# Second-half x operands in four long units, their rests between the halves, scales' one-column matmuls elsewhere, two buffers for down weights

## The chip, the cores and the metric

The kernel runs on one core of a Trainium2 chip. The core has five engines that run side by side and are ordered only by semaphores: TensorE (PE in the profile; its weight loads are PEld), VectorE (DVE), ScalarE (ACT), GpSimd (POOL) and SyncE (SP), which in this kernel issues every DMA. Each engine takes its own instructions in the order in which the program issued them. Matmuls write to eight PSUM banks, and VectorE or ScalarE must read a bank before it can be written anew. The metric is the time of one execution in microseconds, lower is better.

## The reference

Two branches read the same x (2048 rows, 576 columns) and are mixed by a gate:

```python
x = A_x
g = _sigmoid((x * gate_w).sum(-1, keepdims=True))
a = _A_ref(x, A_wq, A_wk, A_wv, A_wo, A_beta)
b = _B_ref(x, B_w_gate, B_w_up, B_w_down)
return g * a + (1 - g) * b
```

Branch A is an attention of 32 heads of size 18 over four segments of 512 rows, with a softmax inside each segment and a running memory matrix from one segment to the next. Branch B is `(silu(x @ w_gate) * (x @ w_up)) @ w_down`, with 4608 inner columns. Everything is in float32, so the kernel splits operands into a high part (the value rounded to a narrower type) and a low part (what the rounding left), and multiplies high with high, high with low and low with high.

## The kernel before, in words

**Projections (0 to about 240 us).** For each of the four segments `s` the kernel makes nine q and k chains (`qk`, chain number `n` from 0 to 8), then eight value groups (`v_step`, group number `n` from 0 to 7) with the memory's matmuls (`mem_step`). `mid` is a list of small work that `qk` issues behind a chain's matmuls. Beside this the kernel measures how large x and the first weights are: squares and peaks are summed up in columns of the tile `sc`; `total` adds such columns, `power` sums over the partitions with a one-column matmul (line 139) into bank 7 and turns the result into a power of two by four small VectorE instructions, and `back` makes the inverse. `sx` is the scale of x; `sw[0]`, `sw[1]` ... are those of groups of four weight tiles. The transposes of the memory update (line 454) and every third value group use bank 7 too.

**Feed-forward (from about 240 us).** The inner columns are cut into 36 tiles, `f` = 0 to 35, and the rows into two halves of 1024. All 36 tiles are worked through for the first half, then for the second: 72 units in a list `seq`, numbered by `pos`. A unit forms gate and up products by Strassen's scheme: seven products (`seven`, `j` = 0 to 6; lines 1188 and 1191) of seven combinations of the weights with seven combinations of x, so 49 matmuls. The last 64 of the 576 columns are handled as a rest, by line 1191. After every third unit the down products of three tiles are due, 16 groups of nine matmuls (line 993, evicted into the sum `ya` by VectorE in line 1002), and they are issued in the following unit, the one with `f % 3 == 0`. That unit is therefore long (about 36 us in the first half), the two behind it are short (about 11). The attention of branch A (`att_gen`: scores in lines 823 and 870, exponentials on ScalarE in line 874, a second part on POOL in line 962) is issued in the long units only while the first half lasts.

**Order of the work.** It is written out by hand. A unit has eight beats (`tick`). `defer(k, fn)` hangs work on the k-th beat from now, so a plan `(o, fn)` in a unit runs at the end of beat `o` (counted from 0; 8 and more lie in the next units). At a beat, what is due goes to its engine's queue in the order in which it was hung there. Between the halves stand ten more beats (`BREAK`), in which nothing but the last 16 down groups is issued.

**What the change touches.** The second half needs its own x operands: for each of seven combinations and two row blocks `z` of the contraction a high part (ScalarE, float16) and a low part (VectorE, line 127), from loaded x tiles that POOL's subtractions (line 1136) combine in place. `x_second` (from `pos` 27) loads four tiles for `z` = 0 and then four for `z` = 1, and spreads the steps over 18 beats each, so over a long unit and the two short ones after it; `parts` issues high and low part in the same beat. `rest_second` (from `pos` 24) does the same for the rests (lines 195 and 196, POOL in line 1159). The raw tiles lie in free places of the x operands' tiles; one of `z` = 1 takes one of the four buffers of `raw_tile`, through which the weights are loaded (`w_load`, line 254). The down weights are loaded by `d_load` (line 259) into the tile `draw`, split by ScalarE and VectorE (`d_split`, lines 974 and 975) and stored.

## Time and profile before

| | |
|---|---|
| median of 3 runs | 1795.76 us (1792.91 to 1799.9) |
| the profiled execution's own time | 1797.75 us |
| its span, first to last instruction | 1795.8 us |
| mean granted TensorE clock | 0.992 |
| PE busy / PEld busy | 1745.5 us (97%) / 1233.4 us (69%) |
| DVE busy / ACT busy / POOL busy | 1347.3 us (75%) / 1005.4 us (56%) / 850.8 us (47%) |
| chain that ended last | PE 78%, DVE 7%, ACT 5% |
| second half's x operands made | in units 24 to 32, 682 to 887 us |

Names in the rows are those of the program: `xo` and `xr` are x tiles (whole ones and rests), `ya` the sum of the down products, `hh` and `hl` the high and low part of a unit's result, `wo__` numbers the weight parts, `kst` and `qst` the attention's keys and queries. A row `A <- B` in the waits says how long engine A stood idle until B's instruction had ended. In a row by stretch, busy time and instruction count stand for each engine, and the clock is the share of full speed that TensorE was granted. A group by line shows busy time and mean nanoseconds of one instruction, and behind the second bar the idle time just before such instructions.

### The profile page before, as it was taken

The numbers are of one execution on the slowest core, as the hardware profiler recorded it, in microseconds if no ns is written. First come the engines' busy times: TensorE is split into PE (matmuls) and PEld (weight loads), VectorE is DVE, ScalarE is ACT, GpSimd is POOL, SyncE is SP. The second block draws the span as 40 slices with busy tenths as digits, with TensorE's granted clock in tenths as the row PEclk, the third lists the DMA queues.
The fourth block names the chain that finished last, engine by engine and source line by source line (L and its number), as shares of the span: only waits on it lengthen the run. The fifth ranks groups of instructions, "written<-read, shape, count | busy, mean of one in ns | idle before, by whom it ended". The sixth has DMA issues, their size and how long they took to land.

```text
span 1795.8 us, 35846 instructions
## 1 busy us (share of the span) xinstructions
PE 1745.5 (97%) x12401; PEld 1233.4 (69%) x12401; DVE 1347.3 (75%) x3339; ACT 1005.4 (56%) x1740; POOL 850.8 (47%) x1065
## 2 busy tenths in 40 slices
PE   9999999999999999988999999999999999999999
PEld 7888856656766676555566757766766766766699
DVE  6768776778878877886775887787877778775455
ACT  7756575767676765664653554455455455455411
POOL 3325551335544554564442555555556555555121
PEclk9999999999999999999999999999999999999999
DMA  8654475776677655544535343354344344333544
GB/s 286 217 189 160 148 250 188 224 224 198 172 239 230 214 174 173 189 134 121 177 115 175 109 147 112 93 156 123 89 134 144 93 120 146 101 103 121 166 143 139
DMA packets 228100, 288.82 MB, mean 161 GB/s; under 512 B 87952, under 2 KB 145168, under 8 KB 227920
## 3 DMA queue, kind: packets, MB, share of 16 engines
q1 hardware_dynamic: 227920, 286.54, 50.3%
q8 instruction: 98, 1.61, 0.4%
q14 instruction: 82, 0.67, 0.1%
HBM read 188.63 MB, written 97.81 MB: 160 GB/s over the span
## 4 chain that ended last, share of the span: by engine, by line
PE 78%; DVE 7%; ACT 5%; issue 3%; DMA 3%; POOL 2%; SPq 1%; DVEq 0%; ACTq 0%; POOLq 0%
PE bank L1188 32%; PE bank L993 23%; PE bank L170 7%; PE bank L1191 5%; PE bank L823 4%; PE bank L870 4%; PE bank L899 2%; PE bank L901 1%; POOL q L399 1%; SPq L936 1%; DMA kst<-stk 1%; DMA rc<-rt 1%; ACT L1181 0%; DMA draw<-in_wd_dram 0%; DVE xo L127 0%
## 5 line engine op out<-in xcount | busy, mean ns | idle before, releaser
L993 PE MATMUL bank<-dw,hh 128*128 128x320 f32 (+1 forms) x2304 | 509.2, 313 | 10.1 <-DVE ya L1002 9.1
L962 POOL TENSOR_TENSOR p<-pe,p 128x512 f16<-128x512 f32 x320 | 386.0, 1206 | 168.7 <-DVE p L960 121.3
L993 PEld LDWEIGHTS bank<-dw,hh 128*128 128x128 f32 x2304 | 380.3, 190 | 35.1 <-DVE ya L1002 10.7
L874 ACT ACTIVATE pe<-bank 128x512 f32<-128x512 f32 x320 | 189.9, 593 | 327.3 <-PE bank L870 289.5
L993 PE MATMUL bank<-dw,hl 128*128 128x320 f32 (+1 forms) x1152 | 341.1, 296 | 1.1 <-DVE hl L123 1.1
L882 POOL TENSOR_SCALAR_AFFINE_SELECT pe<-pe 128x256 f32<-128x256 f32 (+1 forms) x320 | 146.4, 458 | 311.5 <-ACT pe L874 310.0
L830 DVE CUSTOM_DVE_ANT_0 scr<-bank,cm 128x512 bf16<-128x512 f32 (+3 forms) x512 | 248.1, 485 | 26.0 <-PE bank L823 18.0
L1002 DVE TENSOR_TENSOR ya<-bank,ya 128x320 f32<-128x320 f32 x352 | 157.7, 453 | 103.9 <-PE bank L993 101.9
L993 PEld LDWEIGHTS bank<-dw,hl 128*128 128x128 f32 x1152 | 218.4, 190 | 1.6 <-DVE hl L123 1.6
L1191 PE MATMUL bank<-xr,rh 128*128 128x512 f16 x504 | 191.8, 381 | 0.0
L960 DVE CAST p<-pe 128x512 f16<-128x512 f32 x320 | 152.8, 478 | 0.0
L870 PE MATMUL bank<-qst,kst 111*128 111x512 bf16 (+3 forms) x512 | 151.8, 304 | 0.0
L311 POOL TENSOR_TENSOR ws<-raw 128x256 f32<-128x256 f32 x72 | 64.0, 889 | 161.2 <-DMA raw<-in_wf_dram 123.0
L823 PE MATMUL bank<-kst,qst 108*128 108x512 bf16 (+3 forms) x512 | 126.6, 301 | 8.5 <-DMA kst<-stk 5.5
L1092 DVE TENSOR_TENSOR hl<-row,hh 128x512 fp32r<-128x512 f32 x120 | 114.8, 957 | 16.5 <-ACT hh L1091 16.5
L1271 DVE TENSOR_TENSOR row<-bank,row 128x512 f32<-128x512 f32 x72 | 49.7, 691 | 66.3 <-ACT bank L1270 66.1
L1266 ACT ACTIVATE row<-bank 128x512 f32<-128x512 f32 x72 | 43.0, 598 | 94.2 <-PE bank L1191 94.0
L170 PE MATMUL bank<-xo,qhi 128*128 128x512 f32 x288 | 91.9, 399 | 0.3 <-DVE xo L123 0.2
L1270 ACT ACTIVATE bank<-bank 128x512 f32<-128x512 f32 x72 | 41.9, 582 | 89.2 <-PE bank L1191 89.2
L1191 PEld LDWEIGHTS <-rh 128*128 128x128 f16 x504 | 49.5, 98 | 60.1 <-issue 1.3
L399 POOL TENSOR_TENSOR q<-qr,q 128x512 bf16<-128x512 f32 x36 | 48.0, 1332 | 79.1 <-ACT q L398 68.4
L1281 DVE TENSOR_TENSOR row<-bank,row 128x512 f32<-128x512 f32 x72 | 49.6, 689 | 38.4 <-PE bank L1191 29.1
(1050 smaller groups left out, 3826.4 us busy)
## 6 DMA issues: line engine op xcount, KB each, us to landing
xo<-in_wf_dram SPq DMA_DIRECT2D x65, 320.0 KB
dc<-dw SPq DMA_DIRECT2D x36, 576.0 KB
dw<-dc SPq DMA_DIRECT2D x36, 576.0 KB
raw<-in_wf_dram SPq DMA_DIRECT2D x72, 256.0 KB
stk<-q SPq DMA_DIRECT2D x32, 384.0 KB
rh<-rc SPq DMA_DIRECT2D x72, 168.0 KB
draw<-in_wd_dram SPq DMA_DIRECT2D x36, 288.0 KB
xo<-in_xT_dram SPq DMA_DIRECT2D x33, 256.0 KB
```

The costliest lines, as they stand in the source:

```text
L170: nc.tensor.matmul(t, st[n], mv[n], start=(n == 0), stop=(n == 13))
L823: nc.tensor.matmul(t[:, c:c + w], qs[:KR, pr, P * i:P * i + P], ks[:KR, pr, 0:w], start=True, stop=True)
L830: nc.vector.tensor_tensor_reduce(scr[:, :w], t[:, c:c + w], cm[:, L - w:L], 1.0, -3.0e38, OP.add, OP.max, m[:, k:k + 1])
L870: nc.tensor.matmul(t[:, c:c + w], ks[:KR + 3, pr, P * j:P * j + P], qs[:KR + 3, pr, P * j:L], start=True, stop=True)
L874: nc.scalar.activation(pe, t, AF.Exp, scale=SCALE)
L882: nc.gpsimd.affine_select(d, d, pattern=pat, compare_op=OP.is_ge, fill=0.0, base=0, channel_multiplier=-1)
L960: nc.vector.tensor_copy(p1, pe)
L962: nc.gpsimd.tensor_sub(p2, pe, p1)
L993: nc.tensor.matmul(t, p, q[:, cs], start=(f == CH * c and n == 0), stop=(f == CH * c + CH - 1 and n == 2))
L1002: nc.vector.tensor_add(ya[:, i, cs], t, ya[:, i, cs])
L1188: nc.tensor.matmul(t, w[:, p, z], x[z][:, q], start=first and n == 0, stop=False, skip_group_check=True)
L1191: nc.tensor.matmul(t, rem[:, RPOS[j]], XR[j], start=False, stop=True, skip_group_check=True)
```

## The change

1. `x_second(new, z)` is called for `z` = 0 and 1 and returns two plans each. The four plans are hung on the long units 24, 27, 30 and 33, and none of their steps lies beyond beat 7. High and low part are separate steps, the low one a beat or more after the high one. The tile that took a `raw_tile` buffer takes the free tile `xr0`.
2. `rest_second` starts in unit 35 and runs to the seventh of the ten beats between the halves. Its raw tiles come from `raw_tile`, by four loads of 256 KB in place of two of 512 KB. High and low part are separate steps here too.
3. `power(sx)` goes from chain 8 to behind value group 1 of segment 1. `total`, `power` and `back` of `sw[0]` go from segment 2 (chains 0 and 2) to behind value groups 2 and 5 of segment 1. `power` and `back` of `sw[1]` go from chain 5 to chain 6 of segment 2.
4. `draw` has two buffers in place of one.
5. The scratch output of line 830 (`scr`) is written into `junk`, a tile that stood there for the measuring in the projections; `junk` is cut to the size used.

The order of all other instructions on each engine stays as it was.

```diff
-    junk = consts.tile([P, 640], F16, name="junk")[:, :L]
+    junk = consts.tile([P, L], F16, name="junk")
@@ d_load
-        r = fp.tile([P, D], F32, name="draw", bufs=1)
+        r = fp.tile([P, D], F32, name="draw", bufs=2)
@@ chains of segments 1 and 2
-                if s == 1:
-                    if n == 7:
-                        mid.append(lambda: total(sx, 0, 20))
-                    if n == 8:
-                        mid.append(lambda: power(sx, lone_tile([P, 1])))
+                if (s, n) == (1, 7):
+                    mid.append(lambda: total(sx, 0, 20))
                 if s == 2:
-                    if n in (0, 4):
-                        mid.append(lambda: total(sw[n // 4], 20 + 9 * (n // 4), 29 + 9 * (n // 4)))
-                    if n in (2, 5):
-                        mid.append(lambda: power(sw[n // 4], lone_tile([P, 1])))
-                        mid.append(lambda: back(n // 4))
+                    if n == 4:
+                        mid.append(lambda: total(sw[1], 29, 38))
+                    if n == 6:
+                        mid.append(lambda: power(sw[1], lone_tile([P, 1])))
+                        mid.append(lambda: back(1))
@@ value groups, behind v_step and scan_load
+                if s == 1:
+                    if n == 1:
+                        power(sx, lone_tile([P, 1]))
+                    if n == 2:
+                        total(sw[0], 20, 29)
+                    if n == 5:
+                        power(sw[0], lone_tile([P, 1]))
+                        back(0)
@@ s_bank
-                scr = kp.tile([P, L], BF, name="scr", bufs=1)
-                nc.vector.tensor_tensor_reduce(scr[:, :w], t[:, c:c + w], cm[:, L - w:L], 1.0, -3.0e38,
+                nc.vector.tensor_tensor_reduce(junk.bitcast(BF)[:, :w], t[:, c:c + w], cm[:, L - w:L], 1.0, -3.0e38,
@@ x_second, the old steps (24 beats from z = 0 to z = 1)
-            def parts(z, j):
-                new[j][z] = x_home(1, j, z)
-                split_16(new[j][z][:, 0], new[j][z][:, 1], r[z, (0, 0, 3, 2, 1, 3, 2)[j]], sx)
-            steps = [(3, 0, 0), (4, 1, 1), (4, 0, 5), (5, 1, 4), (6, 0, 4), (7, 0, 1), (8, 1, 2), (10, 0, 3), (12, 0, 2),
-                     (13, 1, 6), (17, 0, 6)]
@@ x_second, the new ones (plan, beat, step, combination)
+                if z and q == 2:
+                    r[q] = xr_tile(0)
...
+            def high(j):
+                new[j][z] = x_home(1, j, z)
+                nc.scalar.activation(new[j][z][:, 0], source(j), AF.Copy, scale=sx)
+            def low(j):
+                nc.vector.scalar_tensor_tensor(new[j][z][:, 1], source(j), sx, new[j][z][:, 0],
+                                               op0=OP.mult, op1=OP.subtract)
+            for n, o, fn, j in ((0, 0, load, 0), (0, 0, load, 3), (0, 1, load, 1), (0, 1, load, 2),
+                                (0, 3, high, 0), (0, 4, low, 0), (0, 4, high, 5), (0, 5, total, 1), (0, 5, low, 5),
+                                (0, 6, high, 3), (0, 7, total, 4), (0, 7, low, 3),
+                                (1, 1, high, 4), (1, 2, low, 4), (1, 2, total, 2), (1, 3, high, 1), (1, 4, low, 1),
+                                (1, 4, total, 6), (1, 5, high, 2), (1, 6, low, 2), (1, 6, high, 6), (1, 7, low, 6)):
+                plan[n].append((o, lambda fn=fn, j=j: fn(j)))
@@ rest_second
-            todo = [(0, lambda: load(0)), (1, lambda: load(1))]
-            return todo + [(5 + n, lambda j=j: step(j)) for n, j in enumerate((0, 3, -1, 5, -4, 1, -2, 4, -6, 2, 6))]
+                for a in range(2):
+                    rr[b, a] = raw_tile()
+                    nc.sync.dma_start(rr[b, a], xrest[HALF[1][b]][:, a])
...
+            todo = [(0, load, 0), (2, high, 0), (2, high, 3), (3, low, 0), (3, low, 3), (4, load, 1), (6, high, 5),
+                    (6, total, 1), (7, low, 5), (7, high, 1), (8, total, 4), (8, low, 1), (9, total, 2), (9, high, 4),
+                    (10, low, 4), (11, total, 6), (11, high, 2), (12, low, 2), (13, high, 6), (14, low, 6)]
@@ units
-            if pos == 24:
-                XR2 = [None] * 7
-                plan += [(o, fn) for o, fn in rest_second(XR2)]
-            if pos == 27:
-                X2 = [[None, None] for _ in range(7)]
-                plan += x_second(X2)
+            if pos == 24:
+                X2 = [[None, None] for _ in range(7)]
+                second = x_second(X2, 0) + x_second(X2, 1)
+            if 24 <= pos <= 33 and pos % 3 == 0:
+                plan += second.pop(0)
+            if pos == 35:
+                XR2 = [None] * 7
+                plan += rest_second(XR2)
```

More of the change, by code (lines that the diff above doesn't have):

```diff
@@ L1116, in feed, with x_second, load @@
             return [(f // CH, i, hf, hs, ds, half) for i in range(8) for hf in range(2)]
-        def x_second(new):
+        def x_second(new, z):
             r = {}
-            done = []
-            def load(z, q):
+            def load(q):
                 b, kt = ((0, z), (1, z), (0, 2 + z), (1, 2 + z))[q]
                 if z and q == 2:
-                    r[z, q] = raw_tile()
+                    r[q] = xr_tile(0)
                 else:
-                    j = (0, 3, 4, 5)[q] if z == 0 else (2, 1, 0, 6)[q]
+                    j = ((0, 3, 4, 5), (2, 1, 0, 6))[z][q]
@@ L1128, in load, with total @@
                     x_home(1, j, 0)
                     a, b_, _ = PLACE[1][j][0]
-                    r[z, q] = homes[a, b_][:, 2:4].rearrange("p a n -> p (a n)").bitcast(F32)
-                nc.sync.dma_start(r[z, q], xT[HALF[1][b], :, kt])
-            def total(z, j):
-                c, d, e, g = (r.get((z, q)) for q in range(4))
+                    r[q] = homes[a, b_][:, 2:4].rearrange("p a n -> p (a n)").bitcast(F32)
+                nc.sync.dma_start(r[q], xT[HALF[1][b], :, kt])
+            def total(j):
+                c, d, e, g = (r.get(q) for q in range(4))
@@ L1135, in total, with source @@
                 o, p, q = {1: (c, d, c), 4: (d, g, d), 2: (g, g, c), 6: (e, e, g)}[j]
                 nc.gpsimd.tensor_sub(o, p, q)
-            def parts(z, j):
+            def source(j):
+                return r[(0, 0, 3, 2, 1, 3, 2)[j]]
+            def high(j):
                 new[j][z] = x_home(1, j, z)
-                split_16(new[j][z][:, 0], new[j][z][:, 1], r[z, (0, 0, 3, 2, 1, 3, 2)[j]], sx)
-            steps = [(3, 0, 0), (4, 1, 1), (4, 0, 5), (5, 1, 4), (6, 0, 4), (7, 0, 1), (8, 1, 2), (10, 0, 3), (12, 0, 2),
-                     (13, 1, 6), (17, 0, 6)]
@@ L1144, in x_second @@
-            todo = [(24 * z + q // 2, lambda z=z, q=q: load(z, q)) for z in range(2) for q in range(4)]
-            return todo + [(24 * z + o, lambda z=z, j=j, fn=(parts, total)[k]: fn(z, j)) for z in range(2) for o, k, j in steps]
+                nc.scalar.activation(new[j][z][:, 0], source(j), AF.Copy, scale=sx)
+            def low(j):
+                nc.vector.scalar_tensor_tensor(new[j][z][:, 1], source(j), sx, new[j][z][:, 0],
+                                               op0=OP.mult, op1=OP.subtract)
@@ new lines, in x_second @@
+            plan = [[], []]
+            for n, o, fn, j in ((0, 0, load, 0), (0, 0, load, 3), (0, 1, load, 1), (0, 1, load, 2),
[4 more added lines that the diff above has]
+                plan[n].append((o, lambda fn=fn, j=j: fn(j)))
@@ L1147, in rest_second @@
+            return plan
         def rest_second(rest):
@@ L1150, in load, with total, source, high @@
             def load(b):
-                t = x_slot(5, b, F32)
-                nc.sync.dma_start(t, xrest[HALF[1][b]])
-                rr[b, 0], rr[b, 1] = t[:, 0], t[:, 1]
-            def step(j):
-                if j < 0:
-                    c, d, e, g = rr[0, 0], rr[1, 0], rr[0, 1], rr[1, 1]
-                    o, p, q = {1: (c, d, c), 4: (d, g, d), 2: (g, g, c), 6: (e, e, g)}[-j]
-                    nc.gpsimd.tensor_sub(o, p, q)
-                else:
-                    rest[j] = xr_home(1, j)
-                    rest_16(rest[j], rr[((0, 0), (0, 0), (1, 1), (0, 1), (1, 0), (1, 1), (0, 1))[j]])
-            todo = [(0, lambda: load(0)), (1, lambda: load(1))]
-            return todo + [(5 + n, lambda j=j: step(j)) for n, j in enumerate((0, 3, -1, 5, -4, 1, -2, 4, -6, 2, 6))]
+                for a in range(2):
+                    rr[b, a] = raw_tile()
+                    nc.sync.dma_start(rr[b, a], xrest[HALF[1][b]][:, a])
+            def total(j):
+                c, d, e, g = rr[0, 0], rr[1, 0], rr[0, 1], rr[1, 1]
+                o, p, q = {1: (c, d, c), 4: (d, g, d), 2: (g, g, c), 6: (e, e, g)}[j]
+                nc.gpsimd.tensor_sub(o, p, q)
+            def source(j):
+                return rr[((0, 0), (0, 0), (1, 1), (0, 1), (1, 0), (1, 1), (0, 1))[j]]
+            def high(j):
+                rest[j] = xr_home(1, j)
+                nc.scalar.activation(rest[j], source(j), AF.Copy, scale=sx)
+            def low(j):
+                t = rest[j][32:64]
+                nc.vector.scalar_tensor_tensor(t, source(j)[32:64], sx[32:64], t, op0=OP.mult, op1=OP.subtract)
+            todo = [(0, load, 0), (2, high, 0), (2, high, 3), (3, low, 0), (3, low, 3), (4, load, 1), (6, high, 5),
+                    (6, total, 1), (7, low, 5), (7, high, 1), (8, total, 4), (8, low, 1), (9, total, 2), (9, high, 4),
+                    (10, low, 4), (11, total, 6), (11, high, 2), (12, low, 2), (13, high, 6), (14, low, 6)]
+            return [(o, lambda fn=fn, j=j: fn(j)) for o, fn, j in todo]
         def glance(i, k):
```

## The prediction

> **What bounds the kernel now.** I read the page first, then busy time by stretch, then the waits inside the stretch that stands out.

> ```profile
> PE 1745.5 (97%) x12401; PEld 1233.4 (69%) x12401; DVE 1347.3 (75%) x3339; ACT 1005.4 (56%) x1740; POOL 850.8 (47%) x1065
> ```

> TensorE is busy for 97% of 1795.8 us. A reordering that leaves its matmuls alone can win only its idle time and what its clock loses, so the question is where these lie. I cut the feed-forward's first half into its units at the ScalarE copy of line 1256 (columns: stretch, length, busy time of PE, PEld, DVE, ACT and POOL with instruction counts, granted clock, DMA share, GB/s). Rows: long unit 21, short units 22 and 23; then 24, 25-26, 27, 28-29, 30, 31-32, 33, 34; last, unit 35 with the stretch between the halves.

> ```profile
> 623.97:660.17 36.20, 35.96 (x303) 28.60 (x302) 28.10 (x84) 21.57 (x43) 19.89 (x28) 1.00 0.60 180
> 660.17:682.09 21.92, 21.92 (x104) 10.12 (x103) 18.31 (x30) 18.39 (x31) 10.25 (x11) 1.00 0.68 231
> 682.09:722.50 40.41, 37.82 (x303) 29.99 (x302) 31.45 (x85) 17.27 (x29) 22.20 (x29) 0.96 0.48 137
> 722.50:750.33 27.83, 24.11 (x102) 10.12 (x101) 24.01 (x28) 21.30 (x35) 14.90 (x14) 0.94 0.54 188
> 750.33:788.84 38.51, 36.29 (x303) 28.71 (x302) 33.81 (x88) 18.40 (x31) 22.55 (x29) 1.00 0.43 129
> 788.84:813.76 24.92, 22.34 (x103) 9.69 (x102) 20.57 (x26) 20.46 (x34) 13.76 (x14) 1.00 0.62 203
> 813.76:861.57 47.81, 40.35 (x303) 30.34 (x302) 32.67 (x88) 18.49 (x31) 22.17 (x30) 0.89 0.40 116
> 861.57:887.28 25.71, 22.44 (x102) 9.71 (x101) 20.19 (x26) 20.22 (x33) 13.24 (x13) 1.00 0.57 196
> 887.28:922.99 35.71, 35.71 (x303) 28.54 (x302) 28.72 (x83) 15.51 (x26) 18.28 (x24) 1.00 0.31 100
> 922.99:934.09 11.10, 11.10 (x53) 5.07 (x52) 8.36 (x11) 9.47 (x15) 5.35 (x6) 1.00 0.49 162
> 934.09:964.50 30.41, 29.79 (x192) 23.85 (x191) 14.93 (x28) 8.41 (x15) 0.00 (x0) 1.00 0.50 177
> ```

> Units 21-23 take 58.12 us with 0.24 us of idle PE. Units 24 to 32, with the same 303 and about 103 matmuls, take 205.19: 30.8 above 3 x 58.12. Of this the long units hold 126.73 - 3 x 36.20 = 18.1 and the short ones 78.46 - 3 x 21.92 = 12.7. Those nine units are where the second half's x operands are made; 33 and 34, which make none, are back at 35.71 and 11.10.

> PE idles there for 205.19 - 183.35 = 21.8 us. The rest is the clock (same columns; the first row is from the attention's projections, for later):

> ```profile
> 91.67:98.50 6.83, 5.45 (x23) 5.45 (x24) 3.20 (x13) 1.79 (x4) 1.49 (x1) 0.50 0.42 141
> 706.07:709.48 3.41, 3.41 (x16) 3.08 (x16) 2.55 (x11) 1.21 (x2) 1.56 (x2) 0.50 0.38 124
> 729.96:733.38 3.42, 3.42 (x10) 1.18 (x9) 3.41 (x5) 2.02 (x4) 2.46 (x3) 0.50 0.00 0
> 832.36:835.78 3.42, 3.42 (x12) 1.51 (x11) 2.34 (x8) 2.12 (x3) 1.77 (x3) 0.50 0.33 68
> 849.43:856.26 6.83, 4.95 (x16) 2.87 (x17) 2.17 (x5) 1.82 (x3) 1.53 (x2) 0.50 0.55 147
> ```

> Each is a stretch at half clock behind a gap of about 2 us or more, and loses half its length: 17.08 / 2 = 8.5 in the nine units. 21.8 + 8.5 = 30.3 of the 30.8. So a stall of 2 us costs nearly 4.

> What PE, DVE and SP wait for in those nine units (us in total, times, longest):

> ```profile
> PE bank L993 <- DVE ya L1002: 8.5, 6, 2.6
> PE bank L1188 <- DVE bank L1263: 6.4, 4, 2.0
> PE bank L823 <- DMA kst<-stk: 3.8, 1, 3.8
> ...
> DVE xo L127 <- ACT xo L126: 6.2, 6, 1.6
> DVE xr L196 <- ACT xr L195: 5.5, 3, 3.3
> ...
> SPq L259 <- DVE dw L975: 17.0, 5, 6.3
> SPq L254 <- POOL pe L882: 10.4, 1, 10.4
> ```

> PE waits for VectorE's evictions, and VectorE for ScalarE: a low part stands in VectorE's queue in the same beat as its high part in ScalarE's, so VectorE stands still until ScalarE has come round. One case in order (DVE, DVE, PE; start, length, in brackets the idle time before):

> ```profile
> 704.07 0.74 DVE L196 SCALAR_TENSOR_TENSOR xr<-xo,sc,xr 32x512 f16<-32x512 f32 x1 [3.30 <-ACT xr L195]
> 704.85 0.42 DVE L1002 TENSOR_TENSOR ya<-bank,ya 128x256 f32<-128x256 f32 x1
> 705.32 0.51 PE L993 MATMUL bank<-dw,hh 128*128 128x256 f32 x2 [2.14 <-DVE ya L1002]
> ```

> **The change, part by part.** *x operands.* Nothing is added: 14 + 7 high parts, as many low ones and 12 subtractions stay; only the rests' two loads become four of half the size.

> ```profile
> L127 DVE SCALAR_TENSOR_TENSOR xo<-xo,sc,xo 128x512 f16<-128x512 f32 x10 | 9.7, 967 | 3.2 <-ACT xo L126 3.2
> L126 ACT ACTIVATE xo<-xo,sc 128x512 f16<-128x512 f32 x12 | 8.5, 712 | 0.0
> L196 DVE SCALAR_TENSOR_TENSOR xr<-xo,sc,xr 32x512 f16<-32x512 f32 x7 | 8.4, 1194 | 5.6 <-ACT xr L195 5.5
> L1136 POOL TENSOR_TENSOR xo<-xo,xo 128x512 f32<-128x512 f32 x7 | 10.3, 1473 | 0.0
> ```

> Before, 10 of the 21 low parts fall in long units and 11 in short ones, where VectorE has only 21.92 - 18.31 = 3.6 us to spare in two units. After, the short units have none: I take them at 21.92, all 12.7 us won. Long units 24, 27, 30 and 33 get 3, 4, 3 and 4 low parts, each a beat or more (about 4.5 us) after its high part, so VectorE no longer stands waiting. That adds at most 4 x 0.97 = 3.9 us to VectorE's 28.10 of 36.20, 4 x 0.71 = 2.8 to ScalarE's 15.51 and 2 x 1.47 to POOL's 18.28: all hidden behind PE's 36 us. If that cover failed, the price is the rivals' below. I leave 0.5 us a long unit: -30.8 + 3 x 0.5 = -29.3 for units 24-32 and +0.5 for 33.

> On SP's queue, the load that borrowed a weight buffer goes to a buffer of its own. The 10.4 us wait of the weight load (L254), behind which the attention's keys stood (PE's 3.8), goes with it; that gain is inside the 30.8. The other x loads take free buffers, two or more beats ahead of their readers.

> *The rests* move to unit 35 and the stretch after it: 7 high parts (5 us) and 7 low ones (at 0.74 to 1.2 us, 5 to 8), in 30.41 us where ACT works 8.41, DVE 14.93 and POOL nothing. One place is tight: between unit 35's last products and the down matmuls.

> ```profile
> 943.84 0.68 DVE L1282 TENSOR_TENSOR row<-row 128x512 f32<-128x512 f32 x1
> 944.62 0.69 DVE L123 TENSOR_TENSOR hl<-row,hh 128x512 fp32r<-128x512 f32 x1
> 945.37 0.41 PE L993 MATMUL bank<-dw,hl 128*128 128x320 f32 x1 [0.17 <-DVE hl L123]
> ```

> Two low parts now stand between the first two rows, and PE already waits for the second. Two times 0.75 is +1.5 us (0 if ScalarE is late anyway, 4 with a half-clock stretch behind it). The second pair of rest loads waits for weight buffers that unit 35 frees; behind it on SP stand a down-weight store and the second half's first weight fetches, whose readers start 20 us later: nothing.

> *Scales.* In the projections PE takes one-column matmuls (line 139) in the middle of chains whose values are not ready, then waits for the bank that they occupy:

> ```profile
> 90.66 0.35 PE L139 MATMUL bank<-sc 128*128 128x1 f32 x2 [2.21 <-DVE sc L136]
> 93.05 3.25 PE L170 MATMUL bank<-vw,xo 128*128 128x288 f32 x12 [2.04 <-DVE sc L140]
> 127.01 0.35 PE L139 MATMUL bank<-sc 128*128 128x1 f32 x2 [0.38 <-DVE kt L456]
> 129.95 0.33 PE L454 MATMUL bank<-idt,ph 128*128 128x128 f32 x1 [0.82 <-DVE sc L140]
> 144.22 0.35 PE L139 MATMUL bank<-sc 128*128 128x1 f32 x2 [0.84 <-DVE kt L456]
> ```

> These are 6.29 us of idle PE, and 6.83 / 2 = 3.41 at half clock behind the first two: 9.7. After, the first stands behind the second value group, its sum long done; the second behind the sixth; the third where the transposes no longer use bank 7. The first may find bank 7 still being read from the first value group, with the memory matmuls queued behind it. No row shows that wait: bounds 0 and the 2.04 above, and I take 0.5, since VectorE needs about that once the group has ended. Sum: -9.2.

> *Second buffer for down weights.* SP no longer waits at L259 (17.0 us in these units). Outside units 24-32 only one late down weight reaches PE, in unit 7:

> ```profile
> 376.65 0.77 ACT L974 ACTIVATE dw<-draw,sc 128x576 fp32r<-128x576 f32 x1 [2.44 <-DMA draw<-in_wd_dram]
> ```

> SP reached that load late because of the DMAs ahead of it, not because of its buffer, so I take 0. Bounds: -4.2 (these 2.44 us and a half-clock stretch) to +1, should earlier loads get in others' way. *Scratch:* the mask-and-maximum writes the same bytes into another buffer that VectorE alone writes: 0.

> Sum: -29.3 + 0.5 + 1.5 - 9.2 = -36.5. The profiled execution took 1797.75 us, 2.0 above the median 1795.76 of the runs shown: 1761.2 against the one, **1759.3** against the other.

> **Rivals.** *The long units keep their stalls.* The wait may come with each low part and not from its standing beside the high one. Without the keys' gap and the half-clock stretch after it (3.8 + 3.4) the long units' 18.1 is 10.9 for ten low parts, 1.09 each; 14 cost 15.3 in place of my 2.0: 1772.6. For it: six of the waits for line 1002 lie in long units. Against it: 11.7 us of VectorE's waits for high parts go.

> *The half-clock stretches stay.* They follow gaps of only 2.0 to 2.6 us, but for one. If the gaps are not their cause, 3.41 + 3 x 1.71 = 8.5 us remain: 1767.8. [...] The trace disagrees: every stretch at 0.50 follows such a gap.

> *Slower.* Every low part in a long unit delays an eviction as at 704: 2.14 us of idle PE and 1.71 of half clock, 3.85 each. 14 give 53.9 in place of 2.0: 1811. It makes the kernel slower from 2.75 us a low part on. For it: VectorE would be at 32 of 36 us. Against it: unit 27, with four of them, lost 2.3 in all.

> *It does not do what it says:* the nine units are late for their attention or weight work, and only the scales gain, about 1788. Against it: units 21-23 do the same work without loss.

> **How the numbers follow.** Forecast 0.68, long units keep stalls 0.17, half clock stays 0.04, slower 0.06, no effect 0.05. The first three are faster by over 0.5% (9 us, about what a measurement of this kernel tells from no change): 0.89; same 0.05; slower 0.06. Low end: no residue, no wait behind unit 35 or in the value groups (-4.0) and the down-weight bound (-4.2): 1751. High end: the first rival with the 4 us at unit 35: 1776.

> **What would show it.** Units 24-33 at 58 to 59 us for three, clock 1.00 in all of them; no L254 wait of 10 us; no idle PE ahead of line 139; a wait of 1 to 2 us near the start of the stretch between the halves. Wrong if idle PE behind line 1002 stays in long units, or shows behind the splits between the halves.

## The result, and the profile after

The changed kernel takes 1777.2 us in the median of 4 runs (1775.32 to 1778.46), the kernel before 1794.95 us in the median of 4 runs beside it (1792.91 to 1799.9): a ratio of 0.9896, with a 95% interval from 0.9874 to 0.9919. So it is about 1% faster. The forecast was 1759.3 with a range of 1751 to 1776: the sign was right, half of the gain was missing, and the time lies above the range.

The profiled execution of the changed kernel took 1775.32 us, its span is 1773.1 and the mean granted clock 0.998. From the page of after:

```profile
PE 1735.2 (98%) x12401; PEld 1230.3 (69%) x12401; DVE 1346.9 (76%) x3339; ACT 1004.1 (57%) x1740; POOL 854.8 (48%) x1065
```

Busy time by stretch of after, cut into the same units at the same ScalarE copy (now line 1281). Rows: units 21, 22-23, 24, 25-26, 27, 28-29, 30, 31-32, 33, 34, and unit 35 with the stretch between the halves; the last row lies inside the one before it.

```profile
619.60:655.79 36.19, 35.95 (x303) 28.60 (x302) 28.58 (x84) 21.56 (x43) 19.63 (x28) 1.00 0.60 184
655.79:677.69 21.90, 21.90 (x104) 10.08 (x103) 17.90 (x30) 18.36 (x30) 9.80 (x11) 1.00 0.71 232
677.69:715.41 37.72, 36.52 (x303) 28.64 (x302) 33.19 (x87) 17.77 (x30) 23.38 (x29) 1.00 0.52 148
715.41:737.18 21.77, 21.77 (x102) 9.90 (x101) 17.82 (x23) 18.26 (x31) 11.60 (x12) 1.00 0.69 232
737.18:775.36 38.18, 36.41 (x303) 28.68 (x302) 32.58 (x88) 18.48 (x32) 22.48 (x29) 1.00 0.36 105
775.36:797.12 21.76, 21.76 (x102) 9.89 (x101) 17.79 (x23) 18.24 (x30) 11.49 (x12) 1.00 0.70 232
797.12:834.84 37.72, 36.52 (x303) 28.66 (x302) 33.20 (x87) 17.77 (x30) 23.33 (x29) 1.00 0.51 148
834.84:856.61 21.77, 21.77 (x102) 9.86 (x101) 17.80 (x23) 18.25 (x30) 12.95 (x13) 1.00 0.70 232
856.61:894.36 37.75, 36.24 (x303) 28.59 (x302) 32.64 (x87) 17.92 (x31) 19.79 (x25) 1.00 0.30 95
894.36:905.46 11.10, 11.10 (x53) 5.07 (x52) 9.17 (x11) 9.46 (x16) 6.28 (x7) 1.00 0.53 181
905.46:941.67 36.21, 31.87 (x192) 25.93 (x191) 23.28 (x35) 13.03 (x23) 6.53 (x4) 0.91 0.49 172
918.33:925.16 6.83, 4.71 (x19) 4.71 (x20) 5.59 (x7) 3.39 (x5) 3.12 (x2) 0.50 0.44 154
```

The short units are clean, with no idle PE at all. The clock stands at 1.00 in every unit from 24 to 34. The four long units that make the operands keep 1.2 to 1.8 us of idle PE each. Unit 35 with the stretch behind it has become 5.8 us longer, with 6.83 us at half clock in it. In all, against the profiled execution of before:

| stretch | before | after | difference | forecast |
|---|---|---|---|---|
| projections, up to unit 0 | 241.34 | 235.08 | -6.3 | -9.2 |
| units 0 to 23 | 440.75 | 442.62 | +1.9 | 0 |
| units 24 to 32 | 205.20 | 178.92 | -26.3 | -29.3 |
| unit 33 | 35.71 | 37.75 | +2.0 | +0.5 |
| unit 35 and the stretch between the halves | 30.41 | 36.21 | +5.8 | +1.5 |
| second half and the end | 831.33 | 831.48 | +0.2 | 0 |
| span | 1795.83 | 1773.15 | -22.7 | -36.5 |

What PE still waits for in units 24 to 32 of after, and the longest wait of SP's queue there (us in total, times, longest):

```profile
PE bank L997 <- DVE ya L1006: 4.0, 8, 1.4
```

```profile
SPq L980 <- DVE dw L979: 21.4, 9, 3.6
```

The first row is the only one of PE in that answer: the waits for line 1263 (now 1288) and for the keys are gone, and the weight load's wait of 10.4 us with them. What is left is VectorE's addition into `ya`. SP no longer stands at the load into `draw`; it stands at the store behind it instead (line 980, 21.4 us in place of 17.0), and no wait of PE in these units comes from it.

One long unit's stall in order, from the timeline of after (unit 27; start, length, in brackets the idle time before):

```profile
763.37 1.53 POOL L966 TENSOR_TENSOR p<-pe,p 128x512 f16<-128x512 f32 x1 [1.34 <-PE bank L828]
763.80 1.65 DVE L1149 SCALAR_TENSOR_TENSOR xo<-xo,sc,xo 128x512 f16<-128x512 f32 x1
765.37 0.48 DVE L1006 TENSOR_TENSOR ya<-bank,ya 128x320 f32<-128x320 f32 x1
765.90 0.56 PE L997 MATMUL bank<-dw,hh 128*128 128x320 f32 x2 [1.37 <-DVE ya L1006]
```

The low part no longer waits for ScalarE; VectorE goes straight on. But it lasts 1.65 us, and the addition that PE waits for stands behind it. And the stretch between the halves, again of after:

```profile
914.16 3.36 POOL L1172 TENSOR_TENSOR raw<-raw 128x512 f32<-128x512 f32 x2 [13.44 <-DMA raw<-in_xr_dram]
915.21 1.18 DVE L1307 TENSOR_TENSOR row<-row 128x512 f32<-128x512 f32 x1
915.88 0.72 ACT L1179 ACTIVATE xr<-raw,sc 128x512 f16<-128x512 f32 x1 [0.49 <-POOL raw L1172]
916.42 2.30 DVE L1183 SCALAR_TENSOR_TENSOR xr<-raw,sc,xr 32x512 f16<-32x512 f32 x2
916.50 0.61 ACT L122 ACTIVATE hh<-row 128x512 fp32r<-128x512 f32 x1
917.17 0.56 PE L997 MATMUL bank<-dw,hh 128*128 128x320 f32 x2 [1.62 <-ACT hh L122]
918.20 3.33 POOL L1172 TENSOR_TENSOR raw<-raw 128x512 f32<-128x512 f32 x2 [0.69 <-DVE xr L1183]
918.75 1.64 DVE L123 TENSOR_TENSOR hl<-row,hh 128x512 fp32r<-128x512 f32 x1
920.45 0.64 PE L997 MATMUL bank<-dw,hl 128*128 128x320 f32 x1 [2.72 <-DVE hl L123]
```

Two gaps of PE, 1.62 and 2.72 us, stand where before there were two of 0.45 and 0.17. The first is ScalarE's: a high part of a rest stands ahead of `hh`, and had itself waited 0.49 us for GpSimd's subtraction. The forecast had not looked at it. The second is VectorE's: the two low parts take 2.30 us, and `hl` itself 1.64 us in place of 0.69.

### The profile page after: what moved, and what is told of

It reads as the page before. It is cut to its first block, busy times and chain, and to the rows that moved or that the text cites. A ratio compares the mean times of both kernels' runs of the same rounds, so it can differ in the third digit from the quotient of the medians.

```text
span 1773.1 us, 35861 instructions
## 1 busy us (share of the span) xinstructions
PE 1735.2 (98%) x12401; PEld 1230.3 (69%) x12401; DVE 1346.9 (76%) x3339; ACT 1004.1 (57%) x1740; POOL 854.8 (48%) x1065
## 3 DMA queue, kind: packets, MB, share of 16 engines
q8 instruction: 98, 1.61, 0.4%
## 4 chain that ended last, share of the span: by engine, by line
PE 79%; DVE 7%; DMA 4%; ACT 4%; issue 2%; SPq 2%; POOL 1%; DVEq 0%; ACTq 0%; POOLq 0%
PE bank L1211 31%; PE bank L997 22%; PE bank L170 9%; PE bank L1214 5%; PE bank L828 4%; PE bank L874 4%; PE bank L903 2%; PE bank L905 1%; SPq L940 1%; DMA draw<-in_wd_dram 1%; DMA xo<-in_wf_dram 1%; DMA rc<-rt 1%; DVE xo L1149 1%; PE bank L443 1%; ACT L1204 1%
## 5 line engine op out<-in xcount | busy, mean ns | idle before, releaser
L834 DVE CUSTOM_DVE_ANT_0 junk<-bank,cm 128x512 bf16<-128x512 f32 (+3 forms) x512 | 247.6, 484 | 23.1 <-PE bank L828 15.2
L311 POOL TENSOR_TENSOR ws<-raw 128x256 f32<-128x256 f32 x72 | 68.3, 949 | 150.9 <-DMA raw<-in_wf_dram 99.9
L170 PE MATMUL bank<-xo,qhi 128*128 128x512 f32 x288 | 91.7, 399 | 0.1
L1214 PEld LDWEIGHTS <-rh 128*128 128x128 f16 x504 | 49.3, 98 | 59.5
```

The source lines that it names most:

```text
L170: nc.tensor.matmul(t, st[n], mv[n], start=(n == 0), stop=(n == 13))
L834: nc.vector.tensor_tensor_reduce(junk.bitcast(BF)[:, :w], t[:, c:c + w], cm[:, L - w:L], 1.0, -3.0e38, OP.add, OP.max, m[:, k:k + 1])
L1214: nc.tensor.matmul(t, rem[:, RPOS[j]], XR[j], start=False, stop=True, skip_group_check=True)
```

## Experiments

Every kernel is the changed one with the edit shown, unless said otherwise. "Unit 24: 37.72" is the length of that stretch in the kernel's profiled execution.

### How far one execution speaks for a kernel

The kernel before once more, for a second trace of it:

> The kernel before once more, for its trace. The prediction took the half-clock stretches of one execution as its own: 17.1 us of them in units 24 to 32 and 6.8 behind the first one-column matmul, 12 us lost. If gaps of 2 us always bring them, they stand there again and units 24 to 32 take 205 us. Rival: whether a gap does it depends on how it lies to the clock's periods; then their sum is another, and units 24 to 32 take 197 to 209 us, the time moving with them.

It took 1797.73 us, with a span of 1795.8. Two rows by stretch of this trace: units 24 to 32, and the same nine units of the first trace of before.

```profile
684.14:886.79 202.65, 179.60 (x1210) 117.02 (x1209) 162.37 (x337) 115.98 (x190) 109.08 (x126) 0.98 0.50 155
```

```profile
682.09:887.28 205.19, 183.34 (x1210) 118.56 (x1209) 162.71 (x337) 116.15 (x190) 108.81 (x126) 0.96 0.49 153
```

Idle PE is about the same (23.1 and 21.9 us), but the time at half clock is 6.83 us here and was 17.08 in the trace that the forecast used. So the rival holds: the gaps stand again, the half-clock stretches only in part, and the nine units take 2.5 us less. Units 0 to 23 took 443.00 us in this trace and 440.75 in the other, so the +1.9 us that the table gives to these units is within what two executions of one kernel differ by.

The changed kernel once more:

> The changed kernel once more, beside the other runs of this call. If its traces scatter only by the clock and by when loads land, the time is 1775 to 1779, the feed-forward starts at 235 us, units 24, 27, 30 and 33 take 37.7 to 38.2 us again and the stretch with unit 35 about 36, while units 0 to 23 move by 1 to 3 us.

It took 1775.85 us (1775.69 to 1777.05, 4 runs) against 1798.01 for the kernel before beside it, a ratio of 0.9882 [0.9867, 0.9897]. By stretch: projections 235.84, units 24 to 32 179.03, unit 33 37.69, unit 35 with the stretch behind it 36.34. What remains in long units and between the halves is the same in both traces; it belongs to the kernel.

### The rests between the halves

All splits and subtractions of `rest_second` but the first two pairs move three or four beats later, behind the splits of unit 35's products:

```diff
-            todo = [(0, load, 0), (2, high, 0), (2, high, 3), (3, low, 0), (3, low, 3), (4, load, 1), (6, high, 5),
-                    (6, total, 1), (7, low, 5), (7, high, 1), (8, total, 4), (8, low, 1), (9, total, 2), (9, high, 4),
-                    (10, low, 4), (11, total, 6), (11, high, 2), (12, low, 2), (13, high, 6), (14, low, 6)]
+            todo = [(0, load, 0), (2, high, 0), (2, high, 3), (3, low, 0), (3, low, 3), (4, load, 1), (10, high, 5),
+                    (10, total, 1), (11, low, 5), (11, high, 1), (12, total, 4), (12, low, 1), (13, total, 2), (13, high, 4),
+                    (14, low, 4), (15, total, 6), (15, high, 2), (16, low, 2), (16, high, 6), (17, low, 6)]
```

> The changed kernel, with the rests' steps from the fifth on put behind the splits of the last unit's result (beats 10 to 17 in place of 6 to 14; loads and the first two rests as they are). Theory: the 5.8 us that unit 35 and the stretch after it lost come from two high and two low parts that stand ahead of those splits on ScalarE and VectorE; then that stretch falls from 36.2 back to 30.4 to 31 us and the kernel from 1777.2 to about 1772. Rival: the four loads through the weight buffers, or the rests' work in that stretch as such, cost it; then it stays within 1 us of 1777.2, with 35 to 36 us there.

Measured: 1772.52 us (1771.74 to 1776.69, 4 runs), ratio 0.9869 [0.9854, 0.9883]. From its trace, unit 35 with the stretch behind it, and the two gaps of PE left in it:

```profile
906.56:938.35 31.79, 29.78 (x192) 23.83 (x191) 22.44 (x35) 12.94 (x23) 5.92 (x4) 1.00 0.55 192
```

```profile
917.11 0.56 PE L997 MATMUL bank<-dw,hh 128*128 128x320 f32 x2 [0.45 <-ACT hh L122]
919.23 0.41 PE L997 MATMUL bank<-dw,hl 128*128 128x320 f32 x1 [1.55 <-DVE hl L123]
```

The stretch falls from 36.21 to 31.79 us and the half clock is gone, so where the rests stood was the cause of 4.4 of the 5.8 us. The other 1.4 us is the second gap: in this trace `hl` (line 123) still takes 1.76 us, beside a pair of GpSimd subtractions of line 1172 that runs from 915.22 for 3.41 us.

### The scales

The calls of `total`, `power` and `back` stand where they stood before; all else as in the changed kernel.

```diff
-                if (s, n) == (1, 7):
-                    mid.append(lambda: total(sx, 0, 20))
+                if s == 1:
+                    if n == 7:
+                        mid.append(lambda: total(sx, 0, 20))
+                    if n == 8:
+                        mid.append(lambda: power(sx, lone_tile([P, 1])))
...
-                if s == 1:
-                    if n == 1:
-                        power(sx, lone_tile([P, 1]))
...
```

> The changed kernel, with the scales' sums and one-column matmuls where they were before. By the prediction's sum the move is worth 9.2 us: 1786.4. By the two traces, in which the feed-forward starts at 241.3 and at 235.1 us, it is worth 6.3: 1783.5. Rival: a part of this was a half-clock stretch that depends on how the gaps lie to the clock's own periods, and VectorE, late in the segment after it, gives the rest back; then 3 us or less: at most 1780.

Measured: 1780.87 us (1778.79 to 1781.94, 4 runs), ratio 0.9906 [0.989, 0.9923]; the projections are back at 241.85 us, with 6.83 us at half clock. So the move is worth 6 to 6.8 us against the two traces of the changed kernel and 3.7 to 5.0 between medians (against 1777.2 and 1775.85); by ratios alone the intervals overlap. The trace of after is a lucky one here. Eight of the traces have these projections, and they take 234.64 to 237.55 us: in the five slower ones a half-clock stretch follows the longest of the waits shown next, and in after none does. Where the rest of the forecast's 9.2 us stayed is seen in after's own trace, PE in the projections:

```profile
93.59 0.35 PE L139 MATMUL bank<-sc 128*128 128x1 f32 x2 [1.16 <-DVE dn L492]
105.90 1.35 PE L170 MATMUL bank<-vw,xo 128*128 128x290 f32 x8 [0.61 <-DVE sc L140]
157.91 1.86 PE L170 MATMUL bank<-vw,xo 128*128 128x288 f32 x12 [2.59 <-DVE r L419]
```

Behind value group 1 the bank is still being read, and PE waits 1.16 us where I took 0.5. The bank is then held until group 6 wants it, 0.61 us. And a wait for VectorE that was 0.91 us in the trace of before is 2.59 us. It came with the move: with the scales back it is 0.90. In segment 2, to which this wait belongs, PE first wins 3.1 us on before by the waits that are gone, and at this wait loses 2.0 of them again. It is no fixed bound of VectorE's, for in the kernel with three mends, below, PE comes there 2.7 us earlier still and waits 2.58 again. Why VectorE is late there stays open.

### The second buffer for down weights

```diff
-        r = fp.tile([P, D], F32, name="draw", bufs=2)
+        r = fp.tile([P, D], F32, name="draw", bufs=1)
```

> The changed kernel with one buffer for the down weights, as before the change. The prediction gave the second buffer 0 (between -4.2 and +1): within 1.5 us of the changed kernel beside it. Rival, by units 0 to 23 of the two first traces (480.8 us before, 482.6 after): the second buffer lets loads get in each other's way and costs 2 us; then this is 2 us faster. Second rival: SP's waits at line 259, back again, hold up weights, and it is 2 us or more slower.

Measured: 1776.59 us (1775.2 to 1777.48, 4 runs), ratio 0.9886 [0.9869, 0.9903], beside 0.9882 for the changed kernel. The buffer is worth nothing that can be measured. The late down weight in unit 7 is there with either: ScalarE's split waits 2.57 us for it with one buffer (at 369.77), 2.19 us with two (at 370.51).

### The long units

First, what letting the low part come a beat later is worth. The low parts go back to the beat of their high parts, in the four long units:

```diff
-                                (0, 3, high, 0), (0, 4, low, 0), (0, 4, high, 5), (0, 5, total, 1), (0, 5, low, 5),
+                                (0, 3, high, 0), (0, 3, low, 0), (0, 4, high, 5), (0, 4, low, 5), (0, 5, total, 1),
...
```

> The changed kernel, with each low part of the x operands in the beat of its high part, as before the change, still in the four long units. Theory: VectorE standing behind ScalarE in the same beat is what stalls PE there; the four long units go from 37.7 to 38.2 us back to 38.5 to 40.4, +3 to +10 us: 1780 to 1787. Rival: the gain came from emptying the short units and from the weight buffer, and the beat between the parts is worth nothing: 1777 to 1778.

Measured: 1780.99 us (1778.25 to 1782.3, 4 runs), ratio 0.9909 [0.9894, 0.9924]. Units 24 and 30 stay where they are (37.68 and 37.69), units 27 and 33 go to 39.41 and 40.37. In these two VectorE stands still for ScalarE's high part for 3.30 us in one place, with the addition that PE waits for right behind the low part; this is the one of unit 27:

```profile
762.24 0.75 DVE L1149 SCALAR_TENSOR_TENSOR xo<-xo,sc,xo 128x512 f16<-128x512 f32 x1 [3.30 <-ACT xo L1146]
```

In units 24 and 30 its longest such wait is 1.1 us. So standing beside the high part costs where four low parts fall into a unit, and not where three do: the forecast's reason held in part. In both units 27 and 33 the longest gap of PE is 2.03 us, yet only unit 33 has a stretch at half clock. Four rows by stretch of this trace, the gap and what follows it in unit 27, then in unit 33:

```profile
761.64:765.05 3.41, 1.67 (x14) 1.55 (x15) 2.78 (x9) 1.04 (x2) 0.82 (x2) 1.00 0.50 154
765.05:768.46 3.41, 3.41 (x60) 3.19 (x59) 3.19 (x13) 1.55 (x3) 1.97 (x3) 1.00 0.02 4
881.10:884.51 3.41, 1.38 (x10) 1.12 (x10) 1.63 (x5) 2.19 (x4) 0.56 (x2) 1.00 0.52 164
884.51:887.92 3.41, 3.41 (x17) 3.09 (x17) 2.43 (x10) 1.21 (x2) 1.56 (x2) 0.50 0.00 0
```

These stretches are cut on a grid that the last section shows.

Next, whether what remains comes from the low parts at all. ScalarE makes a scaled copy in place of each, so what the low words hold is left out:

```diff
-                nc.vector.scalar_tensor_tensor(new[j][z][:, 1], source(j), sx, new[j][z][:, 0],
-                                               op0=OP.mult, op1=OP.subtract)
+                nc.scalar.activation(new[j][z][:, 1], source(j), AF.Copy, scale=sx)
```

> After, with each low part of the second half's x operands made by ScalarE as a scaled copy in place of VectorE's scaled subtraction (so what the low words hold is left out; all counts of matmuls stay). VectorE is relieved of 14 instructions of 0.75 to 1.77 us; ScalarE gets 14 of about 0.71 us (as its high parts take, line 1146). Theory, the low parts on VectorE delay the additions into ya and through them TensorE: units 24, 27, 30 and 33 fall from 37.7, 38.2, 37.7 and 37.8 us to 36.1 to 36.5 each, with no idle above 0.3 us in any, span down by 5 to 6.5 us against after's 1773.1. Rival 1, the delay comes from other work of these units (the subtractions on GpSimd, the high parts on ScalarE): they stay at 37.5 to 38.2. Rival 2, ScalarE becomes late in their place: TensorE's gaps there name ScalarE, units at 37 or more.

Measured: 1770.1 us in one run, span 1768.4. Units 24, 27, 30 and 33 by stretch:

```profile
679.39:715.47 36.08, 35.95 (x303) 28.59 (x302) 30.11 (x84) 19.60 (x33) 22.97 (x30) 1.00 0.53 152
737.24:773.33 36.09, 35.95 (x303) 28.62 (x302) 30.12 (x84) 20.83 (x35) 22.37 (x30) 1.00 0.39 112
795.38:831.39 36.01, 35.83 (x302) 28.48 (x301) 30.03 (x84) 19.60 (x33) 23.09 (x30) 1.00 0.53 152
853.16:889.25 36.09, 35.95 (x303) 28.60 (x302) 29.55 (x83) 20.39 (x34) 19.81 (x26) 1.00 0.32 99
```

All four fall to unit 21's length, with the high parts and GpSimd's subtractions in place. The low parts on VectorE are the whole of what remained: 7.1 us in four units. The span is only 4.7 us shorter than after's, mostly because the projections, which the edit does not touch, took 236.77 us in this execution in place of 235.08, with a half-clock stretch in them.

Why do 14 instructions of 0.75 us cost that? In after, 8 of the 14 last 0.74 to 0.81 us and 6 last 1.65 to 1.77. Each of the six starts 0.4 to 0.5 us behind a GpSimd instruction of line 966 or 1139 that is still running, as at 763.80 above, and ends about 0.55 us behind that instruction's end. The other eight have no GpSimd instruction beside them, or start ahead of it (by 0.6 us where it is one of line 886), or meet one that is nearly over: the low part at 741.02 takes 0.80 us beside one of 0.65 that had started 0.39 earlier. To try it, the subtractions of line 1139 are left out (the combined operands are then plain blocks):

```diff
             def total(j):
-                c, d, e, g = (r.get(q) for q in range(4))
-                o, p, q = {1: (c, d, c), 4: (d, g, d), 2: (g, g, c), 6: (e, e, g)}[j]
-                nc.gpsimd.tensor_sub(o, p, q)
+                pass
```

> After, with the four subtractions on GpSimd that make Strassen's sums of the second half's x operands left out in the long units (line 1139; the operands are then the plain blocks, so part of the computation is changed; high and low parts are still made from them). Theory, a low part that starts beside a GpSimd instruction lasts 1.65 to 1.77 us in place of 0.75: the two that lay beside line 1139 (at 709.91 and 829.35) fall to 0.75 us, the ones beside line 966 (four of them) stay at 1.65; the gap of 0.71 us at 711.37 goes and units 24 and 30 come to about 37.0 us, while units 27 and 33 stay at 38.2 and 37.8. Rival, the long time belongs to the operand that was written by GpSimd rather than to the neighbour: all the 1.77 ones fall and those beside line 966 with them. Rival 2, the low parts' length does not matter for TensorE: units 24 and 30 stay at 37.7.

Measured: 1771.69 us in one run, span 1769.5. Units 24 and 27:

```profile
677.31:713.71 36.40, 36.13 (x303) 28.62 (x302) 31.73 (x87) 17.76 (x31) 20.02 (x27) 1.00 0.53 152
735.48:773.66 38.18, 36.42 (x303) 28.70 (x302) 32.63 (x88) 18.48 (x31) 20.10 (x27) 1.00 0.36 106
```

The two low parts that lay beside line 1139 fall from 1.77 to 0.74 us, and units 24 and 30 from 37.72 to 36.40 and 36.27, by more than expected: a gap of 0.22 us ahead of line 997 went too, and PE's busy time fell by 0.4 us. The four beside line 966 keep 1.65 to 1.66, and units 27 and 33 keep 38.19 and 37.74. What lengthens a low part is the GpSimd instruction beside it. The length alone is not the price: two of these four lie in units 24 and 30 and leave no gap of PE there, the other two leave one of 1.37 us each, in units 27 and 33.

Last, the low part is issued at the end of its beat's work, behind the eviction and not ahead of it:

```diff
+        behind = []
+
         def beat(k=None, half=0):
+            beat_(k, half)
+            while behind:
+                behind.pop(0)()
+
+        def beat_(k=None, half=0):
...
-                nc.vector.scalar_tensor_tensor(new[j][z][:, 1], source(j), sx, new[j][z][:, 0],
-                                               op0=OP.mult, op1=OP.subtract)
+                behind.append(lambda: nc.vector.scalar_tensor_tensor(
+                    new[j][z][:, 1], source(j), sx, new[j][z][:, 0], op0=OP.mult, op1=OP.subtract))
```

> The changed kernel, with the x operands' low parts issued at the end of their beat, behind its down groups and attention, and not at its start (one high part a beat later for it). Theory: what the long units still lose (37.7 to 38.2 against 36.2 us) is a low part in front of the evictions of line 1006; behind them it costs nothing, the four units come to 36.2 to 36.7 and the kernel to about 1771 (-5 to -7). Rival: VectorE is simply too full there, or the low part now delays the next product's eviction; the four units stay at 37.5 or more, within 1.5 us of the changed kernel.

Measured: 1774.1 us (1771.29 to 1775.32, 4 runs), ratio 0.9869 [0.9852, 0.9885]. This is 1.8 to 3.1 us under the changed kernel, in place of 5 to 7. Units 27 and 33 fall to 36.03 and 36.07 us, although each holds a low part of 1.61 us: behind the eviction it costs nothing, as expected. Units 24 and 30 stay at 37.47 and 37.48, about the 37.5 of the rival. The timeline of unit 24 in this kernel shows why those two stay:

```profile
706.62 0.74 DVE L1156 SCALAR_TENSOR_TENSOR xo<-xo,sc 128x512 f16<-128x512 f32 x1
706.85 1.53 POOL L966 TENSOR_TENSOR p<-pe,p 128x512 f16<-128x512 f32 x1 [1.39 <-DVE p L964]
707.28 1.65 DVE L319 SCALAR_TENSOR_TENSOR wo__8684<-ws,sc,wo__8684 128x512 f16<-128x512 f32 x1
709.39 0.56 PE L997 MATMUL bank<-dw,hh 128*128 128x320 f32 x2 [0.99 <-DVE ya L1006]
```

The low part now starts 0.23 us ahead of GpSimd's instruction and takes 0.74 us; the weight's low part behind it (line 319) starts beside it and takes the 1.65. The lengthening passed to the next instruction in the queue.

### The three mends together

Low parts behind the eviction, the rests later, and in the projections `power(sx)` behind value group 4 and that of `sw[0]` behind group 7:

```diff
-                    if n == 1:
+                    if n == 4:
                         power(sx, lone_tile([P, 1]))
...
-                    if n == 5:
+                    if n == 7:
                         power(sw[0], lone_tile([P, 1]))
```

> Three repairs together: low parts at the end of their beat; rests behind the last splits; sx's one-column matmul behind value group 4 and that of sw[0] behind group 7, where bank 7 was read long ago and isn't used by the next group. The third should take away the 1.16 and 0.61 us that PE still waits there: the feed-forward starts at 233.3. If all add up: 1777 - 5 - 4.7 - 1.8 = about 1765.5. If VectorE's backlog gives the scales' part back in the next segment, as it did with the changed kernel, 1767.

Measured: 1765.23 us (1761.86 to 1768.36, 4 runs), ratio 0.9821 [0.9802, 0.9841]: better than the kernel before and the changed one. Projections, units 24 to 32, and unit 35 with the stretch behind it:

```profile
0.00:232.04 232.04, 223.88 (x1305) 196.57 (x1306) 174.06 (x408) 151.88 (x307) 104.86 (x120) 1.00 0.61 208
672.55:849.60 177.05, 174.05 (x1210) 115.65 (x1209) 154.91 (x326) 108.76 (x179) 106.94 (x121) 1.00 0.55 171
896.80:928.59 31.79, 29.79 (x192) 23.84 (x191) 22.42 (x35) 13.04 (x23) 5.91 (x4) 1.00 0.56 196
```

Against after's trace: -3.0, -1.9 and -4.4 us, and -1.7 in unit 33 (36.10), together 11.0 of the span's 13.1. The rest lies in units 0 to 23, whose length differs by that much from run to run. That the median meets the expected 1765.5 is partly luck: the low parts gave 3.6 us in place of 5, the scales 3.0 in place of 1.8, and the profiled execution is the fastest of the four.

## Why the prediction was right and wrong

The miss is 17.9 us between medians. Both signs that the prediction named for being wrong are there: idle PE behind the addition into `ya` stays in the long units, and idle PE shows behind the splits between the halves. Against the profiled execution the sum said -36.5 and -22.4 came, 14.1 too few. The other 3.8 us is the choice of execution: the profiled one of before lay 2.0 us above its median, the profiled one of after 1.9 below its own.

*x operands, short units: right.* Forecast 21.92 each pair, measured 21.76 to 21.77. The stall for the keys, the half-clock stretches in the nine units and the weight load's wait went as forecast, and with them fell the rivals "half clock stays" and "does nothing".

*x operands, long units: the term "I leave 0.5 us a long unit" was mis-sized.* It measured 1.5, 2.0, 1.5 and 2.0 us, 7.1 in place of 2.0, so that three units take 59.5 to 59.9 us and not 58 to 59; the experiment without low parts on VectorE shows that they are all of it. I took the mean of 967 ns for a low part and called it hidden, since VectorE had 8 us to spare in the unit. But a spare share of a unit hides nothing when the addition that frees PE's bank stands right behind. The better row was quoted already: unit 27 of before had four low parts and lost 2.3 us; after it lost 2.0. Nor was 967 ns the length of any typical instruction. In the trace of before they run from 735 to 1664 ns with a median of 748, and the longest has the neighbour that the later ones have:

```profile
776.84 1.54 POOL L962 TENSOR_TENSOR p<-pe,p 128x512 f16<-128x512 f32 x1 [1.38 <-PE bank L901]
777.26 1.66 DVE L127 SCALAR_TENSOR_TENSOR xo<-xo,sc,xo 128x512 f16<-128x512 f32 x1
```

The forecast had not looked at what GpSimd runs beside a low part, nor at which of the two starts first. In the rows the length goes with that: a low part starting 0.43 us behind GpSimd's instruction takes 1.65 us, one starting 0.23 us ahead of it takes 0.74.

The rival "long units keep stalls" missed by more (15.3 us against 7.1) than the forecast (2.0), but its mechanism, a wait that comes with a low part even where it does not stand beside its high part, is the one that remained, at 0.5 us a low part. The rival "slower" failed: no low part cost 3.85 us.

*The rests: the term +1.5 (bounds 0 and 4) was mis-sized; +5.8 came.* Its step "two low parts now stand between the first two rows" was right about the place. It priced them at 0.75 each, while beside GpSimd's subtractions the two took 2.30 and `hl` 1.64 in place of 0.69; and it left out ScalarE's high part ahead of `hh`. GpSimd was called idle there ("POOL nothing"), though the change itself brings the subtractions. The half-clock stretch that the bound of 4 allowed for came as well, with 6.83 us. Moving the rests gave 4.4 back.

*Scales: the term -9.2 was mis-sized; -6.3 came.* The new wait for bank 7 was 1.16 + 0.61 in place of 0.5, and 1.68 us of the gain went into a longer wait for VectorE at 157.91, which the step had not followed. In the traces with a half-clock stretch behind that wait less was left, 3.8 us against before in the worst. "No idle PE ahead of line 139" was wrong. Putting the two calls three and two groups later gave 3.0 of it.

*Half clock.* 8.5 us of the forecast's gain came from 17.08 us at half clock in one execution of before; another had 6.83 in the same units, worth 3.4 by the same count, and took 2.5 us less there. The gaps were the kernel's, the price put on them was one execution's. This is no part of the 14.1 us, which are counted against that same execution.

*Down weights and scratch: right at 0* for the buffer, as the run with one shows. The scratch was not tried alone.

*The high end.* Its terms, the first rival with the 4 us at unit 35, add up to 1775.1 and not 1776; the measured 1777.2 lies above either.

## What to carry to other kernels

When an instruction moves into an engine's slack, look at what stands directly behind it in that queue and who waits for that; spare time elsewhere in the unit does not cover it. Price it by the shortest, median and longest of its group together with what GpSimd runs beside it and which of the two starts first (1.65 us behind it and 0.74 ahead of it, here), and count the work that the change itself brings to GpSimd. In these runs a gap of 2 us cost 2 or nearly 4 (two of 2.03 us in one trace, one with 3.41 us at half clock behind it and one without), so take the price of gaps from more than one execution.

## What the runs showed of the hardware

```profile
153.74:157.15 3.41, 1.58 (x13) 1.46 (x12) 3.33 (x6) 2.16 (x5) 0.94 (x1) 1.00 0.00 0
157.15:160.57 3.42, 2.66 (x21) 2.66 (x21) 3.16 (x12) 2.16 (x6) 1.93 (x3) 1.00 0.74 251
```

```profile
154.04:157.45 3.41, 0.94 (x9) 0.82 (x7) 3.35 (x7) 1.52 (x4) 1.57 (x1) 1.00 0.00 1
157.45:160.87 3.42, 3.30 (x14) 3.31 (x15) 3.16 (x12) 2.63 (x7) 1.45 (x2) 0.50 0.92 313
```

The gap is 2.59 us in the one and 2.58 in the other. In the first, 1.84 us of idle time fall into one window and the clock stays; in the second 2.47, and the next window is at 0.50. Units 27 and 33 of the experiment with low parts in their old beat show the same with two gaps of 2.03 us: 1.74 us of idle time in the one window, with the clock at 1.00 behind it, and 2.03 in the other, with 0.50 behind it. Two gaps within one window counted together in after: the stretch at 918.33 follows a window with 1.62 and 0.60 us of two gaps.

*A VectorE instruction that started beside a running GpSimd instruction ended about 0.55 us behind it.* This is counted in the traces of before and after, for VectorE's instructions on 128 x 512 elements of lines 123, 127, 319, 1092 and 1282 of before (in after 123, 127, 319, 1096, 1149 and 1307) with tiles and no bank as inputs. With no GpSimd instruction beside them they took 0.67 to 0.75 us. In 289 cases a GpSimd instruction had started before and had over 0.2 us left to run: 283 of them ended 0.53 to 0.56 us behind it. Of the other six, two ended 0.55 us behind a second GpSimd instruction that had followed the first, two had started within 0.03 us of GpSimd's, and two stood beside a memset and took 0.74. The rows above show it for lines 127, 1149 and 319: GpSimd ends at 778.38, 764.90 and 708.38, VectorE at 778.92, 765.45 and 708.93. So in these traces the length followed from how long GpSimd still had to run, 1.64 to 1.77 us where it had started about half a us earlier. Beside a GpSimd instruction with one input it was the same: in before the low part at 765.11 takes 0.89 us, behind one of line 882 that runs from 765.01 for 0.45. In the other order it was GpSimd's instruction that ended later: in unit 24 with the low parts behind the evictions, the low part ends at 707.36 and GpSimd's instruction, started 0.23 us behind it, at 708.38; this one takes 1.53 us, while one of the same line takes 1.16 at 767.48 in after, where VectorE starts no such instruction.
